# The two ends of a long VectorE-bound kernel: last blocks on four row groups, outputs with tokens on partitions, and another order of casts and transposes at the start

## The chip, the cores and the metric

One core of one Trainium2 chip (trn2). The metric is the device time of one execution in microseconds, the lower the better. Executions of one kernel mostly differ by one to three microseconds here (three of the kernel before took 723.6 to 725.4 us), so every comparison below is between executions taken in turn on the same chip. The "span" is the time from the first to the last instruction of a profiled execution. The device time is about 2 us longer.

"E" is the end of the 132 full multiplies of the last batch. It splits the run into a start (to the first multiply), a middle (first multiply to E) and an end (E to the end of the span).

## The reference

Four batches of 12,416 tokens with 128 channels. In each batch 32 inducing vectors attend to the tokens, which gives h. The tokens then attend to h, and the result goes through a gated feed-forward layer with 1,536 hidden units.

```python
def mab(q, kv):
    s = scale * (q @ kv.transpose(0, 2, 1))
    s = s - s.max(-1, keepdims=True)
    a = np.exp(s)
    a /= a.sum(-1, keepdims=True) + 1e-09
    return a @ kv
h = mab(I, x)            # 32 x 128 for each batch
y = mab(x, h)            # 12416 x 128 for each batch

gate = np.maximum(y @ w_gate, 0.0)
val = y @ w_val
out = gate * val @ w_out
```

## The kernel before

The tokens' attention has only 32 columns, so the kernel never forms y. It multiplies h with the two weights once for each batch (`hgv`, 32 rows of gate and 32 of value, each held twice on the partitions). Then it forms gate and value for 512 tokens (a "block") and 128 hidden units with matmuls of only 32 rows (K=32). The exponentials `p2` are the moving operand. They are left unnormalised: gate and value each carry the factor of the softmax's sum, so the output is scaled by 1/sum twice.

A "pair" is two blocks, and a "slot" is one 128-unit tile of one pair. In a slot TensorE makes two gate and two value tiles, ScalarE takes the ReLU of the gates, VectorE multiplies gate by value out of PSUM (one 128x1024 multiply), and TensorE does the output matmuls of an earlier block. A batch has 12 pairs of 12 slots, and one tile of 128 tokens is left over (the remainder: three half-size multiplies). In the last batch the remainder stands ahead of the last pair.

The exponentials of four blocks come from one "quad": a PSUM bank whose four row groups hold one block each, one exponential, and four small transfers that spread the result:

```python
    def s2_quad_exp(ps):
        p2q = st([P, BLK], FP16, "p2q", 2)
        nc.scalar.activation(out=p2q, in_=ps, func=AF.Exp, scale=sm_scale)
        return p2q

    def p2_copies(p2q):

        p2 = [st([P, BLK], FP16, "p2", 4) for _ in range(2)]
        for j in range(2):
            for d in range(2):
                nc.sync.dma_start(
                    out=p2[j][64 * d : 64 * d + 64, :], in_=p2q[64 * j : 64 * j + 64, :]
                )
        return p2
```

In the last pair of the whole run both blocks' values sit in the same row groups, and the output is formed with channels on partitions, copied, transposed by TensorE and scaled:

```python
for u in range(NFF):
    k = u // 6
    yield dict(
        mm=[
            [
                (...,                       # (cut)
                    p2[r : r + 32, :],
                    hgv[r : r + 32, :],
                )
                for d in range(2)           # both matmuls on the row group r
            ]
            for r in (32 * k, 64 + 32 * k)  # gates, values
        ],
        ...
    )

def step(i):                                # last_block: 12 matmuls of 512 columns
    if i == 0:
        c["ps"] = bank(tag, "o_ps")
    nc.tensor.matmul(c["ps"], wo[:, i, :], gv(i), start=(i == 0), stop=(i == NFF - 1))

def evac(at):
    ...                                     # (cut) copy to fp16 in two halves
    extra[at + 1].append(lambda: finish(zz, oT, osb))

def finish(zz, oT, osb):
    for a in (0, h):
        ps = bank("g", "oo_ps", [P, h, P], FP16)
        for t in range(h):
            nc.tensor.transpose(ps[:, t, :], oT[:, (a + t) * P : (a + t + 1) * P], eye16)
        ...                                 # (cut) scale each tile, store the half
```

At the start, the first batch's x comes in 14 parts. Each is cast to fp16 half by GpSimd and half by ScalarE (the one-tile part by VectorE), transposed by TensorE, and used for the scores and for h. The weights' transfers stand behind x in the same queue, and GpSimd casts them.

The softmax here doesn't subtract the row's maximum and nothing guards it: scores larger than these inputs give would overflow.

Of the kernel before, what the change touches and what calls it, by code (L numbers as in the profile page):

```python
# [18 lines left out]
def kernel(  # L19
# [20 lines left out]
    P = 128  # L40
# [131 lines left out]
    def s2_pair_pe(hT, xT, pr):  # L172
        ps = bank("g", "s2_ps")
        for r in range(4):
            nc.tensor.matmul(
                ps[32 * r : 32 * r + 32, :],
                hT[:, 0:M],
                xTs(xT, (2 * pr + r % 2) * TPB, TPB),
                start=True,
                stop=True,  # L180
            )
        return ps

    def s2_pair_exp(ps):
        p2 = st([P, BLK], FP16, "p2", 4)
        nc.scalar.activation(out=p2, in_=ps, func=AF.Exp, scale=sm_scale)
        return p2

    def s2_quad_pe(hT, xT, qd):

        ps = bank("g", "s2_ps")
        for r in range(4):
            nc.tensor.matmul(  # L193
                ps[32 * r : 32 * r + 32, :],
                hT[:, 0:M],
                xTs(xT, (4 * qd + r) * TPB, TPB),
                start=True,
                stop=True,
            )
        return ps  # L200
# [6 lines left out]
    def p2_copies(p2q):  # L207

        p2 = [st([P, BLK], FP16, "p2", 4) for _ in range(2)]
        for j in range(2):  # L210
            for d in range(2):
                nc.sync.dma_start(
                    out=p2[j][64 * d : 64 * d + 64, :], in_=p2q[64 * j : 64 * j + 64, :]
                )
        return p2
# [57 lines left out]

    for j in range(n_parts + 3):
        if j < n_parts:
# [3 lines left out]
            if t1 == NT:  # L279
                nc.vector.tensor_copy(out=dst, in_=x32)  # L280
            else:
                h = (t1 - t0) // 2
                nc.gpsimd.tensor_copy(out=dst[:, 0:h, :], in_=x32[:, 0:h, :])  # L283
                nc.scalar.copy(out=dst[:, h:, :], in_=x32[:, h:, :])  # L284
        if 1 < j < n_parts + 2:
# [28 lines left out]
        if j < n_parts:  # L314
            t0, t1 = parts[j]
            ps = bank("g", "xT_ps", [P, 8, P], FP16)
            for t in range(t0, t1):
                nc.tensor.transpose(ps[:, t - t0, :], x16[:, t, :], eye16)  # L318
            nc.vector.tensor_copy(out=xTs(xT, t0, t1 - t0), in_=ps[:, 0 : t1 - t0, :])  # L319
# [11 lines left out]
    s2 = s2_pair_pe(hT, xT, 0)  # L331
    p2 = s2_pair_exp(s2)
# [40 lines left out]
    def ev_s2_pair(b, pr, first, last):  # L373
        def pe(at):
            ps = s2_pair_pe(state[b]["hT"], state[b]["xT"], pr)

            def act():
                p2s[(b, pr)] = s2_pair_exp(ps)

            post[at + 1].append(act)  # L380
            ev_z2(lambda: p2s[(b, pr)], [(b, pr, k) for k in range(2)], TPB, at + 2)
# [3 lines left out]
    def ev_s2_quad(b, qd, first, last):  # L385
        def pe(at):
            ps = s2_quad_pe(state[b]["hT"], state[b]["xT"], qd)
# [71 lines left out]
    for b in range(B):  # L459
        for qd in range(NPAIR // 2):  # L460
            base = slot(b, 2 * qd, 0)
            if base:

                a = base - 2 * NFF if qd else slot(b - 1, NPAIR, 0) - 14
                ev_s2_quad(b, qd, a + 4, a + 8)
            else:
                ev_s2_pair(b, 1, 5, 8)
# [165 lines left out]
    def chain(w, gv, key, k, t0, first):  # L633
# [43 lines left out]
        if w == BLK:  # L677
            steps = [(first if i == 0 else 0, lambda i=i: step(i)) for i in range(NFF)]
            fast = key[0] == B - 1 and key[1] > NPAIR - 5
            counts = (5, 5) if fast else (6, 5)  # L680
# [6 lines left out]
    extra = defaultdict(list)  # L687

    def last_block(gv, key, k, t0, tag, on_act):
        c = {}  # L690
        h = TPB // 2

        def step(i):
            if i == 0:
                c["ps"] = bank(tag, "o_ps")
            nc.tensor.matmul(c["ps"], wo[:, i, :], gv(i), start=(i == 0), stop=(i == NFF - 1))  # L696

        def evac(at):
            z = z2is[key + (k,)][:, :, 0]
            zz = st([P, TPB], FP32, "zz", 2)  # L700
            nc.vector.tensor_tensor(out=zz, in0=z, in1=z, op=ALU.mult)
            oT = st([P, BLK], FP16, "oT", 4)
            osb = st([P, TPB, P], FP32, "osb", 4)
            for a in (0, h):
                nc.scalar.copy(out=oT[:, a * P : (a + h) * P], in_=c["ps"][:, a * P : (a + h) * P])
            extra[at + 1].append(lambda: finish(zz, oT, osb))

        def finish(zz, oT, osb):
            for a in (0, h):
                ps = bank("g", "oo_ps", [P, h, P], FP16)  # L710
                for t in range(h):
                    nc.tensor.transpose(ps[:, t, :], oT[:, (a + t) * P : (a + t + 1) * P], eye16)
                for t in range(h):
                    sc = zz[:, a + t : a + t + 1]
                    if on_act:
                        nc.scalar.activation(
                            out=osb[:, a + t, :], in_=ps[:, t, :], func=AF.Copy, scale=sc
                        )
                    else:
                        nc.vector.tensor_scalar(  # L720
                            out=osb[:, a + t, :],
                            in0=ps[:, t, :],
                            scalar1=sc,
                            scalar2=None,
                            op0=ALU.mult,
                        )
                nc.sync.dma_start(
                    out=ov[key[0]][:, t0 + a : t0 + a + h, :], in_=osb[:, a : a + h, :]
                )

        return step, evac
# [3 lines left out]
    def units():  # L735
        for b in range(B):
            for pr in order(b):
                base = slot(b, pr, 0)
                p2, hgv = p2s[(b, pr)], state[b]["hgv"]
                if (b, pr) == (B - 1, NPAIR - 1):  # L740
                    gvs = [st([P, 6, 2, BLK], FP16, "gv", 4) for _ in range(2)]
                    for k in range(2):
                        step, evac = last_block(
# [4 lines left out]
                            "og"[k],  # L748
                            k == 0,
                        )  # L750
                        if k == 0:
                            steps = [(base + 8, lambda i=i, f=step: f(i)) for i in range(NFF)]
                            job(steps, evac, ([3, 3, 3, 3],) * 2)
                        else:
                            for i in range(NFF):
                                a = base + 12 + (i + 2) // 4
                                extra[a].append(lambda i=i, f=step: f(i))
                            extra[base + 15].append(lambda f=evac: f(base + 16))
                    for u in range(NFF):
                        k = u // 6  # L760
                        yield dict(
# [8 lines left out]
                                    for d in range(2)  # L770
                                ]
                                for r in (32 * k, 64 + 32 * k)
                            ],
                            dst=gvs[k][:, u % 6, :, :].rearrange("p k c -> p (k c)"),
                        )
                elif pr < NPAIR:
# [14 lines left out]
                    for s in range(NFF):  # L791
                        if s % 6 == 0:
# [14 lines left out]
                            dst=gvs[-1][:, s % 6, :, :].rearrange("p k c -> p (k c)"),  # L807
                        )
# [49 lines left out]
    while True:  # L858
# [4 lines left out]
        if not (unit or any(window) or ready or fills or post or jobs or extra):  # L863
# [7 lines left out]
        if ready and at >= 10:  # L871
# [5 lines left out]
        if ready and at < 10:  # L877
# [46 lines left out]
        for f in extra.pop(at, []):  # L924
            f()
# [5 lines left out]
        if ready:  # L931
            n = ready["dst"].shape[-1]
            nc.vector.tensor_tensor(  # L933
                out=ready["dst"], in0=ready["g16"][:, 0:n], in1=ready["v"][:, 0:n], op=ALU.mult
            )
# [31 lines left out]
```

## Time and profile before

| | before |
|---|---|
| device time, median of 3 runs | 719.7 us (718.93 to 719.73) |
| span of the profiled execution | 716.4 us |
| first multiply starts | 28.67 us |
| 132 full multiplies of the last batch | 149.48 us, 1.132 us each |
| E to the last multiply's end | 18.26 us |
| E to the end of the span | 24.15 us |

The profile's page gives busy time by engine and then groups of equal instructions. The timeline gives runs of equal instructions of one engine in order: start, length, engine, source line, operation, tiles, count, and in brackets the idle time before and what ended it. It draws equal instructions into one line over waits shorter than 0.15 us, so a line without a bracket can still hold short waits. The last table row is what the change aims at: 24.15 us in which VectorE is not at its own pace or is done. The first multiply's start is its other aim. The lines themselves are in the prediction.

### The profile page before, as it was taken

How to read it: one execution, taken by the hardware profiler on the slowest of the kernel's cores; microseconds unless marked ns; L12 is line 12 of the kernel's file. 1: busy time of each engine (PE TensorE's matmuls, PEld its weight loads, DVE VectorE, ACT ScalarE, POOL GpSimd, SP SyncE). 2: the span in 40 equal slices, each digit the busy share in tenths (PEclk: the TensorE clock that was granted, in tenths of full speed). 3: DMA queues.
4: the chain of work that ended last, by engine and by line, in shares of the span. 5: the costliest groups of instructions: out<-in, count | busy, mean ns of one | idle time of the engine just before them, and what ended most of it. 6: DMA issues, size and time to landing. Idle time of an engine off the chain costs nothing.

```text
span 716.4 us, 13907 instructions
## 1 busy us (share of the span) xinstructions
PE 639.5 (89%) x4554; PEld 191.1 (27%) x4554; DVE 684.5 (96%) x630; ACT 679.6 (95%) x1378; POOL 343.3 (48%) x621
## 2 busy tenths in 40 slices
PE   5999999998988999998898999999888898898997
PEld 5422222222222222222222222222222222222222
DVE  4699999999999999999999999999999999999996
ACT  5799999999999999999999999999999999999985
POOL 3574536561365546626163662754325451551531
PEclk9999999999999999999999999999999999999999
DMA  9656677531346978522147766762122133232222
GB/s 344 219 125 177 150 181 163 103 89 45 91 126 166 195 164 223 126 67 76 46 107 206 170 155 170 170 118 75 59 68 83 56 90 67 67 88 67 67 68 72
DMA packets 142489, 87.76 MB, mean 122 GB/s; under 512 B 116913, under 2 KB 125905, under 8 KB 140113
## 3 DMA queue, kind: packets, MB, share of 16 engines
q1 hardware_dynamic: 142416, 86.88, 46.8%
q8 instruction: 35, 0.57, 0.3%
q14 instruction: 38, 0.30, 0.1%
HBM read 27.80 MB, written 25.43 MB: 74 GB/s over the span
## 4 chain that ended last, share of the span: by engine, by line
PE 44%; ACT 23%; issue 15%; DVE 15%; DMA 3%; SPq 0%; POOL 0%; DVEq 0%; ACTq 0%
PE o_ps L640 19%; ACT g L930 16%; DVE gv L933 14%; PE v_ps L830 14%; PE g_ps L830 7%; ACT oT L646 6%; DMA gv<-in_x_dram 2%; PE s_ps L193 1%; PE o_ps L696 1%; PE s1T_ps L511 1%; ACT p1T L521 0%; PE idle_ps L272 0%; DMA p1g<-p1T 0%; ACT hgv L166 0%; PE xT_ps L318 0%
## 5 line engine op out<-in xcount | busy, mean ns | idle before, releaser
L933 DVE TENSOR_TENSOR gv<-g,v_ps 128x1024 f16<-128x1024 f16 x576 | 660.8, 1213 | 10.7 <-PE g_ps L830 6.8
L930 ACT ACTIVATE g<-g_ps 128x512 f16<-128x512 f32 x1164 | 613.3, 620 | 16.6 <-PE g_ps L830 8.6
L640 PE MATMUL o_ps<-gv,wo 128*128 128x512 f16 x1128 | 339.8, 383 | 36.8 <-ACT oT L646 36.6
L657 POOL TENSOR_SCALAR osb<-o,z2i 128x128 f32<-128x128 f16 x380 | 164.6, 447 | 275.0 <-DMA o<-oT 251.3
L830 PE MATMUL g_ps<-p,hgv 32*128 32x512 f16 x1152 | 284.8, 380 | 5.3 <-ACT g L930 1.7
L830 PE MATMUL v_ps<-p,hgv 32*128 32x512 f16 x1152 | 226.2, 383 | 11.5 <-DVE gv L933 9.7
L830 PEld LDWEIGHTS <-hgv 32*128 32x128 f16 x2400 | 73.6, 91 | 271.5 <-issue 267.3
L640 PEld LDWEIGHTS <-wo 128*128 128x128 f16 x1176 | 79.2, 97 | 192.0 <-issue 169.1
L436 POOL TENSOR_TENSOR z2i<-zt,minus 128x16 f32<-128x16 f32 (+2 forms) x29 | 72.5, 2501 | 1.5
L646 ACT CAST oT<-o_ps 128x512 f16<-128x512 f32 (+1 forms) x98 | 57.1, 583 | 0.4 <-PE o_ps L640 0.4
L490 POOL CAST x<-x 128x2048 f16<-128x2048 f32 x18 | 34.0, 1890 | 19.4 <-DMA x<-in_x_dram 15.0
L429 POOL TENSOR_TENSOR zt<-zt 128x128 f32<-128x128 f32 (+5 forms) x116 | 33.4, 288 | 9.1
L595 POOL TENSOR_TENSOR hp<-hp,hq 128x129 f32<-128x129 f32 (+1 forms) x18 | 8.2, 457 | 32.5 <-ACT hq L594 27.9
L429 POOL TENSOR_TENSOR zt<-p2T 128x256 f32<-128x256 f16 (+2 forms) x29 | 17.0, 586 | 9.3 <-DMA p2T<-p2q 7.0
L319 DVE COPY xT<-xT_ps 128x1024 f16<-128x1024 f16 (+1 forms) x13 | 8.5, 650 | 7.2 <-PE xT_ps L318 6.4
L204 ACT ACTIVATE p2q<-s_ps 128x512 f16<-128x512 f32 x23 | 15.1, 656 | 0.0
L283 POOL CAST x<-gv 128x512 f16<-128x512 f32 (+1 forms) x13 | 7.5, 580 | 12.3 <-DMA gv<-in_x_dram 12.2
L284 ACT CAST x<-gv 128x512 f16<-128x512 f32 (+1 forms) x13 | 7.5, 580 | 6.1 <-DMA gv<-in_x_dram 6.1
L521 ACT ACTIVATE p1T<-s1T_ps 128x512 f16<-128x512 f32 x18 | 12.2, 677 | 0.0
L318 PE MATMUL xT_ps<-eye,x 128*128 128x128 f16 x97 | 9.6, 256 | 2.1 <-POOL x L283 1.5
L193 PE MATMUL s_ps<-xT,hT 128*32 128x512 f16 x92 | 9.2, 387 | 1.9
L291 ACT ACTIVATE p<-s_ps 128x256 f16<-128x256 f32 (+2 forms) x14 | 5.0, 354 | 4.9 <-PE s_ps L289 4.8
(90 smaller groups left out, 162.1 us busy)
## 6 DMA issues: line engine op xcount, KB each, us to landing
out_dram<-osb SPq DMA_DIRECT2D x94, 256.0 KB, 2.2
x<-in_x_dram SPq DMA_DIRECT2D x18, 1024.0 KB, 5.8
p<-p2q SPq DMA_DIRECT2D x92, 64.0 KB, 2.0
gv<-in_x_dram SPq DMA_DIRECT2D x11, 512.0 KB, 7.5
o<-oT SPq DMA_TRANSPOSE x98, 2.3
x<-in_moe_w_out_dram SPq DMA_DIRECT2D x1, 768.0 KB, 9.1
gv<-in_x_dram SPq DMA_DIRECT2D x2, 256.0 KB, 10.7
x<-in_moe_w_gate_dram SPq DMA_DIRECT2D x1, 512.0 KB, 9.2
```

Of the source, the lines that this page charges most:

```text
L193: nc.tensor.matmul(ps[32 * r : 32 * r + 32, :], hT[:, 0:M], xTs(xT, (4 * qd + r) * TPB, TPB), start=True, stop=True,)
L204: nc.scalar.activation(out=p2q, in_=ps, func=AF.Exp, scale=sm_scale)
L429: nc.gpsimd.tensor_tensor(out=dst, in0=v[:, :, :, 0:m], in1=v[:, :, :, m : 2 * m], op=ALU.add)
L436: nc.gpsimd.tensor_tensor(out=z2i, in0=v[:, :, :, 0], in1=minus1[:, 0 : n * g].rearrange("p (n g) -> p n g", n=n), op=ALU.pow,)
L490: nc.gpsimd.tensor_copy(out=s["x16"][:, t0:t1, :], in_=s["x32", q])
L521: nc.scalar.activation(out=p1T, in_=ps, func=AF.Exp, scale=sm_scale)
L640: nc.tensor.matmul(c["ps"][:, 0:w], wo[:, i, :], gv(i), start=(i == 0), stop=(i == NFF - 1))
L646: nc.scalar.copy(out=oT[:, 0:w], in_=c["ps"][:, 0:w])
L657: nc.gpsimd.tensor_scalar(out=osb[:, t, :], in0=o16[:, t, :], scalar1=zz, scalar2=zz, op0=ALU.mult, op1=ALU.mult,)
L830: nc.tensor.matmul(ps[:, cols], hgv[:, s * P : (s + 1) * P], p2, start=True, stop=True)
L930: nc.scalar.activation(out=g16[:, k * BLK : (k + 1) * BLK], in_=ps, func=AF.Relu)
L933: nc.vector.tensor_tensor(out=ready["dst"], in0=ready["g16"][:, 0:n], in1=ready["v"][:, 0:n], op=ALU.mult)
```

## The change

Its intent:

1. **Four row groups in the last pair.** Each of the last two blocks is laid out on all four row groups, so the two gates and two values of a slot can run at once. To get that layout without transfers, the last quad becomes three banks with three exponentials.
2. **Tokens on partitions.** The last two blocks' outputs take gv as the stationary operand (four matmuls of 128 columns in place of one of 512). The result needs no transposition, only scaling: GpSimd scales the first block, VectorE the second with two multiplies.
3. **The start.** The last part of x is cast by GpSimd alone and transposed earlier. A filler matmul follows each of the first twelve parts, to keep TensorE's clock up. The first multiply is split in two, and its value matmuls are issued ahead.
4. **"Even last chains".** The output matmuls of the blocks before the last ones are spread over 6 slots rather than 5, except those of the very last such block, which are done in 4.

```diff
@@ the last quad of p
-                ev_s2_quad(b, qd, a + 4, a + 8)
+                if b == B - 1 and qd == NPAIR // 2 - 1:
+                    bl = 2 * NPAIR - 4
+                    ev_s2(b, (b, 2 * qd), (bl, bl + 1, bl, bl + 1), a + 4, a + 8)
+                    for k in range(2):
+                        ev_s2(b, (b, 2 * qd + 1, k), (bl + 2 + k,) * 4, a + 16 + 6 * k, a + 20 + 6 * k)
+                else:
+                    ev_s2_quad(b, qd, a + 4, a + 8)
@@ the last pair's matmuls
-                                    for d in range(2)
+                                    for d, r in ((0, 64 * j), (1, 64 * j + 32))
                                 ]
-                                for r in (32 * k, 64 + 32 * k)
+                                for j in range(2)
                             ],
@@ the last two blocks' outputs
-            nc.tensor.matmul(c["ps"], wo[:, i, :], gv(i), start=(i == 0), stop=(i == NFF - 1))
+            for t in range(TPB):
+                nc.tensor.matmul(
+                    c["ps"][:, t, :],
+                    gv(i)[:, t * P : (t + 1) * P],
+                    wo[:, i, :],
+                    start=False,
+                    stop=(i == NFF - 1 and t == TPB - 1),
+                )
... (cut: copies, scaling and stores of the two blocks)
@@ the start
+            if j == n_parts - 2:
+                t0, t1 = parts[j + 1]
+                nc.gpsimd.tensor_copy(out=x16[:, t0:t1, :], in_=x32s[j + 1])
...
+        if j < n_parts - 1:
+            turn(j)
+        if j == n_parts - 2:
+            turn(j + 1)
+        elif j < n_parts - 2:
+            idle(z1_ps[:, BLK : 2 * BLK], 1, xTs(xT, parts[0][0], 4).rearrange("p t c -> p (t c)"))
@@ the multiply
+            w = n // ready.get("parts", 1)
+            for a in range(0, n, w):
+                nc.vector.tensor_tensor(...)      # parts=2 in slot 0 and in the very last slot
@@ chains
-            fast = key[0] == B - 1 and key[1] > NPAIR - 5
-            counts = (5, 5) if fast else (6, 5)
+            counts = (6, 5)
+            if key[0] == B - 1 and key[1] == NPAIR - 2:
+                counts = (6, 5) if k == 0 else (4, 4)
```

## The prediction

> **What bounds the kernel now.** I read the page's busy times first, then the groups, then VectorE in order of time, and last the two ends of the run.
>
> ```profile
> PE 639.5 (89%) x4554; PEld 191.1 (27%) x4554; DVE 684.5 (96%) x630; ACT 679.6 (95%) x1378; POOL 343.3 (48%) x621
> L933 DVE TENSOR_TENSOR gv<-g,v_ps 128x1024 f16<-128x1024 f16 x576 | 660.8, 1213 | 10.7 <-PE g_ps L830 6.8
> L930 ACT ACTIVATE g<-g_ps 128x512 f16<-128x512 f32 x1164 | 613.3, 620 | 16.6 <-PE g_ps L830 8.6
> ```
>
> VectorE does one multiply per slot, 576 in all, and waits 10.7 us before them in the whole run. ScalarE's 95% is less tight than it looks: ten ReLUs in a row took 5.00 us at the start (timeline from 27.42 us), so (5.00 - 0.60) / 9 = 0.49 us each, 0.98 us a slot. VectorE in order of time settles it:
>
> ```profile
> 542.76 149.48 DVE L933 TENSOR_TENSOR gv<-g,v_ps 128x1024 f16<-128x1024 f16 x132 [0.58 <-PE g_ps L830]
> 692.16 0.68 DVE L933 TENSOR_TENSOR gvr<-g,v_ps 128x512 f16<-128x512 f16 x1
> 693.10 1.28 DVE L933 TENSOR_TENSOR gvr<-g,v_ps 128x512 f16<-128x512 f16 x2 [0.26 <-PE g_ps L830]
> 695.16 8.75 DVE L933 TENSOR_TENSOR gv<-g,v_ps 128x1024 f16<-128x1024 f16 x7 [0.78 <-ACT g L930]
> 704.27 3.81 DVE L933 TENSOR_TENSOR gv<-g,v_ps 128x1024 f16<-128x1024 f16 x3 [0.36 <-PE g_ps L830]
> 708.15 2.35 DVE L933 TENSOR_TENSOR gv<-g,v_ps 128x1024 f16<-128x1024 f16 x2
> ```
>
> The last batch's 132 multiplies run without a gap: (149.48 - 1.21) / 131 = 1.132 us a slot, VectorE's own pace. Nothing in the change makes that multiply cheaper, and it is over 90% of the span. Only the two ends can give: before the first multiply (28.67 us), and from 692.25 us (end of the 132), when the one-tile remainder and the last pair of blocks run. There the slot is longer: 12 multiplies from 695.16 to 710.50 us are 15.34 us, 1.28 us each.
>
> The reason for 1.28 is on TensorE, and after the last multiply a chain follows:
>
> ```profile
> 695.66 0.38 PE L830 MATMUL v_ps<-p,hgv 32*128 32x512 f16 x1
> 695.89 0.37 PE L830 MATMUL v_ps<-p,hgv 32*128 32x512 f16 x1
> 696.20 0.82 PE L640 MATMUL o_ps<-gv,wo 128*128 128x512 f16 x3
> 710.14 1.46 PE L696 MATMUL o_ps<-gv,wo 128*128 128x512 f16 x6
> 711.63 0.65 ACT L705 CAST oT<-o_ps 128x256 f16<-128x256 f32 x2 [0.22 <-PE o_ps L696]
> 712.44 1.13 DVE L720 TENSOR_SCALAR osb<-oo_ps,zz 128x128 f32<-128x128 f16 x4 [1.87 <-PE oo_ps L712]
> 713.08 0.85 SPq L727 DMA_DIRECT2D out_dram<-osb  x2
> ```
>
> The two value matmuls share a row group and start 0.23 us apart, as the gates do. So the four take 0.54 us (695.66 to 696.20), the three output matmuls 0.75, a slot 1.29. In a slot of the pair before, all four started at 684.64 and the outputs at 684.97: 0.33 us, slot 1.08. The last matmuls end at 711.60, 1.10 us after the last multiply; copy, transposes, scaling and store then take 4.8 us to 716.4.
>
> **What the Trainium skill says.** (1) "TensorE: Matmul & The Clock Gate", Part 3 (packing small matmuls): K=32 matmuls in different row groups run concurrently, in one row group they don't; the trace agrees, 0.33 against 0.54 us. (2) Same page, "Back-to-back issue gap": 56 ns for an isolated 128-column matmul, about 81 in a sustained stream with weight loads. The change swaps 12 512-column matmuls for 48 128-column ones, so this decides. Here the remainder's output matmuls took 0.38 us for 4 and 0.62 for 8: 60 ns each with its weight load. I use 56 to 60. (3) "VectorE: DVE Perf Modes", the perf-mode tier table: a tensor_tensor with a PSUM operand gets the 1x mode, so 1,024 elements at that page's 0.96 GHz are 1.07 us; the trace's 1.13 agrees. (4) The first page again, Part 1: TensorE falls to half clock after an idle window of about 3.4 us. The trace grants 0.50 over 21 to 23 us, after 1.28 us of idle that ended at 18.78.
>
> **The change part by part.**
>
> *Start.* The last quarter-megabyte of x is cast wholly by GpSimd (0.61 instead of 0.40 us in parallel), ScalarE loses a 0.40 us cast, and the part's transposes move ahead of the scores of the part before. Filler matmuls (0.22 us each) after each part may keep TensorE at full clock. hT_ps now ends at 25.0. Following the order, the reshuffle alone brings that to about 24.4, with the full clock about 23.8. But what follows needs w_val's second cast:
>
> ```profile
> 25.12 1.04 POOL L327 CAST wv<-x 128x1024 f16<-128x1024 f32 x1 [0.64 <-DMA x<-in_moe_w_val_dram]
> 26.29 0.38 PE L156 MATMUL hgv_ps<-wv,hT 128*32 128x512 f16 x2
> 27.19 1.28 DVE L340 CAST hgv<-hgv_ps 128x512 f16<-128x512 f32 x2
> ```
>
> It waits for a transfer and ends at 26.16; the matmuls that read it start at 26.29 now, so they can move by under 0.1 us. The gain left lies behind them: VectorE's first copies (0.75 us) can now be done before 26.3, so the second copies start at about 26.7 to 26.9 instead of 27.19. The first multiply, split in two and with its values issued earlier, need not sit out the 0.21 us for ScalarE. Two halves cost about 0.07 more than one (two 128x512 multiplies took 1.28, one whole 1.21). Net: 0.30 to 0.50 + 0.2 - 0.07, I take **0.45 us**. The rest of the 0.6 to 1.2 us becomes idle time before the weights.
>
> *Middle.* The last quad of p becomes three exps in place of one: two more on ScalarE, about 0.55 us each, while their DMA copies go. ScalarE's spare time is 1.13 - 0.98 = 0.15 us a slot, less one 0.5 us copy every six slots: 0.07 net, near 5 us over the last 70 slots. Spreading chains over 6 slots instead of 5 changes nothing where VectorE has no gap. Cost 0 to 0.3 us, I take **0.1 lost**.
>
> *Remainder and last pair.* Let E be the end of the last full multiply, 692.25 now. The first of the last pair starts at E + 2.91. In the new order each remainder slot has 2 output matmuls instead of 3, then 3, and the chain's next matmul waits for ScalarE's copy of the single output bank, which stands behind two ReLUs. Laying the slots out I get E + 2.8, so 0.1 saved. With four row groups a slot on TensorE is 0.33 + 0.75 = 1.08, or 0.33 + 12 x 0.056 + 0.1 = 1.10, just under VectorE's 1.132. Early on there are two slots of four output matmuls (1.30) and two more bank waits; I charge 0.8 us. So 11 x 1.132 + 1.28 (last one halved) + 0.8 = 14.5: the last multiply ends at E + 17.3, against E + 18.25 (710.50). **0.95 saved.**
>
> *After the last multiply.* The second block's chain can't start until the first block's sum has left the one output bank and the last value matmuls are issued, about 2.1 us before the last multiply ends. It needs 0.22 + 48 x 0.056 + 0.2 = 3.1 us: it ends 1.0 to 1.1 us after the last multiply. That equals the 1.10 of before. With tokens on partitions, two VectorE multiplies remain: 128x256 from PSUM, an estimate of 0.43 + 0.33 from hT's 0.23 us for 64 columns and the 1x pace. The first store is issued at +0.5, the second at +0.95 (0.43 each). Now the second store is issued near 713.5 and the span ends 2.9 us later; same size, same 2.9. So 0.95 + 2.9 = 3.85 instead of 4.8: **0.95 saved.** GpSimd's four scalings for the first block (0.60 each from fp32, as its one such instruction took) end about 0.5 us before they could block the last store.
>
> Sum: 0.45 - 0.1 + 0.95 + 0.95 = 2.25; the run-to-run spread of 0.8 us covers the rounding. **719.7 - 2.25 = 717.4 us**; I say 717.2, as the start is taken carefully.
>
> **Rivals.** *The start pays in full:* if the weights' transfers land earlier, since the last cast is moved, 0.6 to 1.2 us come through and the time is near 716. Against it: they wait in the same queue, and w_val's cast waits 0.64 us on it. *The last pair becomes perfectly VectorE-bound:* no bank waits, 0.8 us more, 716.3. For it: single waits under 0.6 us vanish in buffers in the steady part; against it: the chain of the second block has one bank. *TensorE becomes the bound:* at 81 ns a 12-matmul slot is 1.40 us, costing 0.27 x 4, and the final 48 cost 1.2 more: the tail gains nothing, 719.3. Against it are the 60 ns above. *GpSimd and the queue hold the last store:* the first block's store stands ahead of it in SyncE's queue, with 0.5 us of slack; if GpSimd is 1 us late, 718.
>
> **Range and chances.** Start 0 to 1.2, slots of the last pair 0 to 1.8, tail 0.3 to 1.5 saved; they are independent, so 715.4 to 718.8 should hold it 8 times in 10. Two per cent would be 14.4 us, which neither end contains: faster 0.01, within 0.98, slower 0.01.
>
> **What would show it.** First multiply near 28.2 instead of 28.67, with TensorE idle before the w_val matmuls. A gapless run of about 130 multiplies at 1.132 in the last batch. Last pair's multiplies at 1.13 to 1.2 instead of 1.28, no two matmuls of one slot 0.22 apart. 48 output matmuls in about 2.7 us; under 4 us from their end to the span's. I am wrong if the output matmuls take 80 ns, if gaps appear around the extra exps, or if the start moves by 1 us.

## The result, and the profile after

| | before | changed |
|---|---|---|
| device time, median of 4 runs each | 719.72 us (718.93 to 720.44) | 717.87 us (717.31 to 718.57) |
| span of the profiled execution | 716.4 us | 716.4 us |
| first multiply starts | 28.67 us | 28.67 us |
| first multiply to E | 663.57 us | 665.49 us |
| E to the last multiply's end | 18.26 us | 17.58 us |
| E to the end of the span | 24.15 us | 22.24 us |

The ratio is 0.9975, with a 95% interval of 0.9958 to 0.9992. Ratios are worked out from runs of the same rounds, so a ratio is not quite the ratio of the medians quoted beside it. The change gained 1.85 us by the medians. That is under 2% and so counts as "same", and it lies inside the predicted range.

The two profiled spans are equal by chance. The profiled execution of before took 718.67 us, less than any of the four timed ones. So I compare stages, not spans.

The page of the changed kernel, busy time by engine and the two costliest groups (the multiply is now L953, the ReLU L948):

```profile
PE 639.7 (89%) x4640; PEld 194.7 (27%) x4640; DVE 683.8 (95%) x628; ACT 678.0 (95%) x1372; POOL 350.0 (49%) x639
L953 DVE TENSOR_TENSOR gv<-g,v_ps 128x1024 f16<-128x1024 f16 (+1 forms) x578 | 660.8, 1210 | 11.6 <-PE g_ps L849 8.1
L948 ACT ACTIVATE g<-g_ps 128x512 f16<-128x512 f32 x1164 | 613.1, 619 | 17.3 <-PE g_ps L849 9.4
```

VectorE's multiply takes the same 660.8 us. The page can't show what the change did: idle time before the multiply went from 10.7 to 11.6 us, which alone would read as a loss. VectorE's timeline shows it better:

```profile
28.67 5.81 DVE L953 TENSOR_TENSOR gv<-g,v_ps 128x512 f16<-128x512 f16 x6
...
544.16 150.00 DVE L953 TENSOR_TENSOR gv<-g,v_ps 128x1024 f16<-128x1024 f16 x132 [0.58 <-PE g_ps L849]
...
697.07 8.61 DVE L953 TENSOR_TENSOR gv<-g,v_ps 128x1024 f16<-128x1024 f16 x7 [0.58 <-PE g_ps L849]
705.93 5.81 DVE L953 TENSOR_TENSOR gv<-g,v_ps 128x1024 f16<-128x1024 f16 x6 [0.25 <-issue]
712.73 0.76 DVE L723 TENSOR_TENSOR osb<-o_ps,zz 128x256 f32<-128x256 f32 x2 [1.00 <-issue]
```

Three things are to be seen. The first multiply starts when it did before. The 132 multiplies take 150.00 us, not 149.48. The last pair (now 13 multiplies, as the very last is halved) starts 2.91 us after E and ends 17.58 us after it, with a gap of 0.25 us inside whose releaser is "issue", which means that no wait is seen. The end, TensorE's and SyncE's timeline:

```profile
705.08 0.39 PE L849 MATMUL v_ps<-p,hgv 32*128 32x512 f16 x2
705.40 0.84 PE L709 MATMUL o_ps<-wo,gv 128*128 128x128 f16 x12
706.18 0.39 PE L849 MATMUL v_ps<-p,hgv 32*128 32x512 f16 x2
...
709.79 2.85 PE L709 MATMUL o_ps<-wo,gv 128*128 128x128 f16 x48
...
713.18 0.81 SPq L729 DMA_DIRECT2D out_dram<-osb  x2
```

The values of a slot now start together (0.39 us for two, no second group 0.23 us behind). Twelve output matmuls take 0.84 us, and the slot comes round after 706.18 - 705.08 = 1.10 us, just under VectorE's 1.132. The 48 output matmuls of the last block end at 712.64, 0.90 us after the last multiply (697.07 + 14.67 = 711.74). Two scalings and the two stores follow, and nothing else.

At the start, VectorE and TensorE of the changed kernel:

```profile
17.43 0.61 PE L265 MATMUL xT_ps<-eye,x 128*128 128x128 f16 x8
17.87 0.38 PE L259 MATMUL z_ps<-xT,eye 128*128 128x512 f16 x1
...
18.60 0.61 PE L265 MATMUL xT_ps<-eye,x 128*128 128x128 f16 x8
...
24.24 1.04 POOL L324 CAST wv<-x 128x1024 f16<-128x1024 f32 x1 [0.29 <-DMA x<-in_moe_w_val_dram]
...
25.33 0.36 DVE L142 RECIPROCAL rz<-z_ps 128x32 f32<-128x32 f32 x1 [1.05 <-PE hT_ps L310]
...
26.52 0.38 PE L156 MATMUL hgv_ps<-wv,hT 128*32 128x512 f16 x2
```

One part takes TensorE 18.60 - 17.43 = 1.17 us, of which the filler (L259, 0.22 us from issue to issue) is a fifth. The reciprocal that follows h's last matmul starts at 25.33 us. In before it started at 25.10:

```profile
25.10 0.36 DVE L142 RECIPROCAL rz<-z_ps 128x32 f32<-128x32 f32 x1 [1.05 <-PE hT_ps L313]
```

So h is not earlier but 0.23 us later (and that with the last part of x 0.49 us sooner: its cast starts at 20.29 us, in before at 20.78), although the windows show the full clock that the fillers were meant for. The columns are the window, its length, then busy time and count of PE, PEld, DVE, ACT and POOL, the granted TensorE clock, the DMA share and GB/s. First before, then changed:

```profile
20.00:22.00 2.00, 1.91 (x30) 1.85 (x31) 0.82 (x2) 1.15 (x5) 1.37 (x4) 0.53 1.02 404
22.00:24.00 2.00, 1.99 (x40) 1.74 (x39) 1.13 (x3) 0.78 (x3) 1.25 (x3) 0.62 1.11 329
```

```profile
20.00:22.00 2.00, 2.00 (x47) 1.74 (x45) 1.10 (x2) 1.28 (x4) 1.61 (x4) 1.00 1.02 401
```

Before ran at 0.53 and 0.62 of the clock just where it matters and was still done sooner.

**Half-clock stretches blur everything.** Such a stretch lasts 3.41 us in each trace that has one. It also comes in the middle of a run, at places that differ between traces. In the changed kernel's trace it stands at 253.8 us. Laid slot by slot over a trace without one, it costs 1.27 us (1.25 to 1.29 in six traces). Take it off, and "first multiply to E" is 665.49 - 1.27 = 664.22 us: 0.65 us longer than before, not 1.92.

### The profile page after: what moved, and what is told of

Same layout as the page of the kernel before. It is cut to its first block, busy times and chain, and to the rows that moved or that the text cites. A ratio compares the mean times of both kernels' runs of the same rounds, so it can differ in the third digit from the quotient of the medians.

```text
span 716.4 us, 14081 instructions
## 1 busy us (share of the span) xinstructions
PE 639.7 (89%) x4640; PEld 194.7 (27%) x4640; DVE 683.8 (95%) x628; ACT 678.0 (95%) x1372; POOL 350.0 (49%) x639
## 5 line engine op out<-in xcount | busy, mean ns | idle before, releaser
L953 DVE TENSOR_TENSOR gv<-g,v_ps 128x1024 f16<-128x1024 f16 (+1 forms) x578 | 660.8, 1210 | 11.6 <-PE g_ps L849 8.1
L948 ACT ACTIVATE g<-g_ps 128x512 f16<-128x512 f32 x1164 | 613.1, 619 | 17.3 <-PE g_ps L849 9.4
L436 POOL TENSOR_TENSOR z2i<-zt,minus 128x16 f32<-128x16 f32 (+3 forms) x31 | 73.4, 2367 | 1.6
L429 POOL TENSOR_TENSOR zt<-zt 128x32 f32<-128x32 f32 (+5 forms) x124 | 35.1, 283 | 9.7
L429 POOL TENSOR_TENSOR zt<-p2T 128x256 f32<-128x256 f16 (+3 forms) x31 | 17.5, 564 | 16.3 <-DMA p2T<-p2q 7.7
L175 PE MATMUL s_ps<-xT,hT 128*32 128x512 f16 x108 | 10.8, 387 | 2.4
L953 DVE TENSOR_TENSOR gvr<-g,v_ps 128x512 f16<-128x512 f16 x12 | 8.0, 684 | 1.7 <-PE g_ps L849 1.7
```

The source lines that it names most:

```text
L175: nc.tensor.matmul(ps[32 * r : 32 * r + 32, :], hT[:, 0:M], xTs(xT, blocks[r] * TPB, TPB), start=True, stop=True,)
L429: nc.gpsimd.tensor_tensor(out=dst, in0=v[:, :, :, 0:m], in1=v[:, :, :, m : 2 * m], op=ALU.add)
L436: nc.gpsimd.tensor_tensor(out=z2i, in0=v[:, :, :, 0], in1=minus1[:, 0 : n * g].rearrange("p (n g) -> p n g", n=n), op=ALU.pow,)
L948: nc.scalar.activation(out=g16[:, k * BLK : (k + 1) * BLK], in_=ps, func=AF.Relu)
L953: nc.vector.tensor_tensor(out=ready["dst"][:, a : a + w], in0=ready["g16"][:, a : a + w], in1=ready["v"][:, a : a + w], op=ALU.mult,)
```

## The experiments

Three batches of four kernels, five rounds each. "Clear runs" are executions with a mean granted clock of at least 0.999. This is a cut of mine, and few runs fall in it. Of before, 5 of 33 were clear, with a mean of 718.22 us; the other 28 had 720.19. Of the changed kernel, 5 of 10 were clear (717.56), and the other 5 had 718.33.

| run | median (lowest to highest), us | ratio to before, 95% | clear runs: number, mean us | E to end, us |
|---|---|---|---|---|
| e0_changed_again | 717.94 (717.54 to 718.46) | 0.9963, 0.9934 to 0.9993 | see above | 22.22 |
| e1_start_only | 720.54 (719.04 to 721.80) | 1.0004, 0.9971 to 1.0036 | none | 24.17 |
| e2_end_only | 717.56 (717.36 to 718.23) | 0.9958, 0.9929 to 0.9988 | none | 22.09 |
| e3_no_filler | 717.93 (715.97 to 719.19) | 0.9960, 0.9929 to 0.9991 | 2, 716.57 | 22.24 |
| e4_old_outputs | 718.40 (717.82 to 719.62) | 0.9980, 0.9961 to 0.9999 | 4, 718.33 | 22.73 |
| e5_old_groups | 719.18 (718.16 to 720.38) | 0.9989, 0.9970 to 1.0008 | 2, 718.40 | 23.72 |
| e7_early_exps | 718.08 (717.62 to 718.61) | 0.9973, 0.9953 to 0.9993 | 3, 717.79 | 22.20 |
| e8_no_split | 717.84 (717.17 to 718.39) | 0.9970, 0.9952 to 0.9988 | 3, 717.37 | 22.14 |
| f1_late_filler | 717.45 (715.97 to 718.13) | 0.9975, 0.9962 to 0.9988 | 2, 716.24 | 22.15 |
| f2_copied_blocks | 716.93 (715.75 to 717.31) | 0.9967, 0.9955 to 0.9980 | 1, 715.75 | 22.13 |
| f3_copied_old_start | 716.00 (715.34 to 716.99) | 0.9958, 0.9945 to 0.9971 | 4, 715.83 | 22.12 |
| f4_one_more | 717.77 (717.25 to 718.59) | 0.9985, 0.9972 to 0.9999 | 3, 717.51 | 22.26 |

Before's median in the same rounds was 719.89 us for e0 to e3, 719.86 for e4 to e8 and 718.93 for f1 to f4 (11 runs each). It moved by nearly 1 us between batches, so medians of different batches are not compared. "E to end" is E, taken from VectorE's timeline, subtracted from the end of the profiled span. The page prints the span to 0.1 us, so this column is good to 0.05 us.

### The changed kernel once more

No edit.

> The changed kernel, unaltered, on the same chip and in the same rounds as the others, for a second trace. It should be 1.85 us below the kernel before, as the first comparison gave, give or take 0.6. If the long slots of batches 1 to 3 in its first trace (0.74 us at 255 us, 0.57 at 189, 0.56 at 412) belong to the change, they stand again at the same multiplies (numbers 194, 137, 328); if they are chance, they don't.

717.94 us, again 1.95 us below before. The stages repeat: 132 multiplies in 150.01 us and the last multiply 17.58 us after E. Of the three long slots, those of 0.57 and 0.56 us stand again at the same multiplies, so they belong to the change. The one of 0.74 us does not: it was the half-clock stretch, which is there again, but now at 425 us.

### The start alone

```diff
+ before.py, with the new order of casts and transposes, the fillers,
+ the early values and the split first multiply; the end as before
```

> The kernel before with the start of the change alone. My prediction's step: 0.45 us saved, first multiply near 28.2 us, bounded by the cast of w_val. Rival, from the changed kernel's trace: the filler matmuls make TensorE the bound of the start (1.17 us a part), which takes the saving back: 0.0 us, give or take 0.3, first multiply near 28.7.

The ratio is 1.0004, but its interval is some 2 us wide to each side, too wide to tell 0.45 us from nothing. The trace decides for the rival: the first multiply starts at 28.75 us (28.67 in before) and the reciprocal at 25.41 us (25.33 in the changed kernel, 25.10 in before).

### The end alone

```diff
  the changed kernel, with
- the new order at the start, the fillers, the early values, the split
+ the start of before
```

> The changed kernel with the start of the kernel before. If the start gives nothing, this saves all of the 1.85 us (1.4 to 1.9, with the two exps' 0.5 us in it). If my prediction's 0.45 us for the start holds, it is that much slower than the whole change. In its trace the end of the last multiply should be 17.6 us after the end of the 132 full ones, and the span's end 4.7 us later.

717.56 us, the lowest median of its batch: the times show no part of the gain in the start. By luck its profiled execution kept the full clock at the start, and VectorE's timeline shows the start of before as I had expected it of the change, and the last pair without a wait of 0.15 us or more:

```profile
28.18 8.15 DVE L941 TENSOR_TENSOR gv<-g,v_ps 128x1024 f16<-128x1024 f16 x7 [0.28 <-ACT g L936]
...
696.42 14.33 DVE L941 TENSOR_TENSOR gv<-g,v_ps 128x1024 f16<-128x1024 f16 x13 [0.58 <-PE g_ps L838]
```

The first multiply is at 28.18 us with none of the change's start in it. Its reciprocal came at 24.22 us, and VectorE then waited 0.21 us for the matmuls on w_val's second half. So at full clock w_val's cast does set the first multiply, as predicted, once h is early enough. The changed start, with 28.67 and 28.62 us in its two traces, is a loss of 0.5 us against this.

### No fillers

```diff
-        elif j < n_parts - 2:
-            idle(z1_ps[:, BLK : 2 * BLK], 1, xTs(xT, parts[0][0], 4)...)
```

> The changed kernel without the 12 filler matmuls of the start; all else as in the change. If the fillers bound the start, parts go at the pace of the transfers and the first multiply comes 0.3 to 0.7 us earlier than with them (near 28.1). If they pay because they hold the full clock, TensorE is granted 0.5 from about 20 to 23.5 us again and the start is no earlier or up to 0.5 us later.

The median equals the changed kernel's (717.93 against 717.94), but the spread is wide: 715.97 to 719.19. The two clear runs have 716.57 us, 1.0 less than the changed kernel's clear runs. The profiled one has half the clock from 20.0 to 23.4 us, as before has it, and a reciprocal at 26.18. Its last part of x also came later than in the changed kernel (the cast starts at 21.75 us, not 20.29), so only the time from there can be compared: 4.43 us to the reciprocal here and 4.32 in before, both with the half clock; 4.05 to 5.32 in the eight traces with all fillers, which have none. In two of these, e0 and e4, GpSimd waited for a part of x about as long as in before (1.99 and 1.90 us against 2.01), and the full clock held. So the fillers do prevent the half-clock stretch, and cost about as much as it does.

### Four row groups, outputs as before

```diff
  the changed kernel, with
- last_block: gv stationary, tokens on partitions
+ last_block of before: 512-column matmuls, copy, transposes, scaling
```

> The changed kernel with the last pair on four row groups but its outputs made as before (twelve 512-column matmuls, copy, transposes, scaling). My prediction gives the row groups 0.95 us and the new output path 0.95 us of their own. So: the last pair's multiplies go at 1.13 to 1.2 us a slot, the last one ends 17.2 to 17.6 us after the end of the 132 full ones, but the span ends 5.9 us after that (23.3 after the 132; 22.2 in the change, 24.15 before): about 0.95 us slower than the change. Rival, that the two are worth nothing apart because the output copies hold ScalarE and the banks: 24 us after the 132, 1.8 slower.

E to the end takes 22.73 us, against 24.15 before: the row groups, with the halved last multiply, bring 1.42 us. The last multiply ends 17.47 us after E, as expected; the rest takes 5.26 us and not the expected 5.9.

### New outputs, row groups as before

```diff
  the changed kernel, with
- three banks and exponentials for the last four blocks, r = 64 * j, 64 * j + 32
+ ev_s2_quad and its transfers, both matmuls of a tile on the row group r
```

> The changed kernel with the last pair's p in the old layout (both gates in one row group, both values in another) and the new outputs with tokens on partitions. By my prediction the slot stays at 0.54 + 0.75 us = 1.28 to 1.3, the last multiply ends 18.3 us after the 132, and the span 4.7 us later: 23.0, about 0.8 us slower than the change. The 132 run without the 0.5 us of long slots, if the two extra exps cause these, so the time comes out only 0.3 us above the change.

E to the end takes 23.72 us, where 23.0 was expected: the outputs, again with the halved last multiply, bring 0.43. The two parts together bring 1.91, and 1.42 + 0.43 = 1.85. That looks as if they simply added, but the halved multiply is in both sums, and no run takes it out. The last multiply is *later* than before here, 18.63 us after E against 18.26 (18.3 expected). TensorE's and VectorE's timelines of this run's last pair show why the outputs alone don't pay there:

```profile
704.42 0.38 PE L841 MATMUL v_ps<-p,hgv 32*128 32x512 f16 x1
...
705.73 0.39 PE L841 MATMUL v_ps<-p,hgv 32*128 32x512 f16 x1
...
705.49 5.81 DVE L945 TENSOR_TENSOR gv<-g,v_ps 128x1024 f16<-128x1024 f16 x6 [0.48 <-PE g_ps L841]
```

A slot on TensorE takes 705.73 - 704.42 = 1.31 us, still longer than VectorE's multiply, and VectorE waits 0.48 us on gates. The middle tells something else: with the quad's one exponential back and the new counts kept, the 132 multiplies take 149.54 us. So the half microsecond comes with the three banks, and not with the chains spread over six slots. Each of the two extra banks brings an exponential and four more score matmuls on TensorE; no run takes these apart.

### The two extra exponentials earlier

```diff
-                        ev_s2(b, (b, 2 * qd + 1, k), (bl + 2 + k,) * 4, a + 16 + 6 * k, a + 20 + 6 * k)
+                        ev_s2(b, (b, 2 * qd + 1, k), (bl + 2 + k,) * 4, a + 10 + 6 * k, a + 14 + 6 * k)
```

> The changed kernel with the two last blocks' scores and exps six slots earlier. If the extra exps, standing close to the remainder's exp and the output copies, make the long slots of the last batch (150.0 us for the 132 multiplies instead of 149.5), the 132 come back to 149.5 to 149.7 and the time falls by 0.3 to 0.5 us. If their number counts and not their place, 150.0 stays. If the chains of 4 output matmuls cause it, the long slots stay near the start of the last full pair.

The 132 multiplies take 150.00 us in both places. By the rule set beforehand their number would count and not their place, but the traces say more. Laid multiply by multiply over a trace with one exponential (the copied blocks, below), each trace shows where it falls behind. ScalarE's timeline of the changed kernel, then of this run:

```profile
670.42 0.67 ACT L186 ACTIVATE p<-s_ps 128x512 f16<-128x512 f32 x1
677.49 0.67 ACT L186 ACTIVATE p<-s_ps 128x512 f16<-128x512 f32 x1
```

```profile
664.14 0.67 ACT L186 ACTIVATE p<-s_ps 128x512 f16<-128x512 f32 x1
671.21 0.67 ACT L186 ACTIVATE p<-s_ps 128x512 f16<-128x512 f32 x1
```

In the changed kernel the first of the two, twelve slots after the exponential before it, delays nothing. The multiplies come late from the 119th to the 130th: behind the second, six slots after the first, and behind the remainder's short one, six slots after that (0.46 us in all). In this run both stand six slots after another, and the late ones are the 107th to the 118th. The remainder's, now twelve slots behind, delays nothing. So what costs in these traces is an exponential six slots after another, and not their number. No run sets them all twelve apart.

### The first multiply whole

```diff
-                            parts=2 if base + s == 0 else 1,
```

> The changed kernel with its very first multiply whole again; the filler matmuls stay. Two multiplies (numbers 138 and 329) started 0.36 us late in all four traces with the changed start and in neither without; they lie 384 VectorE instructions apart, and the split is one instruction more. If that shift of one exposes a pause in the supply of instructions, both late starts vanish: 0.7 us faster, less the split's own worth (0.0 to 0.2). If the fillers or the early turn cause them, they stay and the time is unchanged.

The profiled execution has no half-clock stretch, and the last pair takes one unbroken run:

```profile
190.15 8.20 DVE L952 TENSOR_TENSOR gv<-g,v_ps 128x1024 f16<-128x1024 f16 x7 [0.21 <-PE g_ps L848]
...
696.58 14.33 DVE L952 TENSOR_TENSOR gv<-g,v_ps 128x1024 f16<-128x1024 f16 x13 [0.58 <-PE g_ps L848]
```

The last multiply ends 17.24 us after E instead of 17.58. At 190 us, the multiply that waits 0.57 us in the changed kernel waits 0.21 here; before has 0.21 too. The times do not show it (in the profiled execution GpSimd waited 3.00 us for an early part of x, and the first multiply came only at 29.63 us): 717.84 us against 718.08 of the run with early exponentials and 717.94 of the changed kernel, and 717.37 against 717.56 in the clear runs.

### One more instruction, nothing split

The split can matter in two ways: as two halves, or as one more VectorE instruction ahead of all others. This tells them apart.

```diff
-                            parts=2 if base + s == 0 else 1,
+    spare = constp.tile([P, 1], FP16, name="spare")
+    nc.vector.memset(spare, 1.0)          # among the constants
```

> The changed kernel without the split of the first multiply (whose run had no late multiplies), plus one tiny VectorE instruction (a memset of one column) among the constants at the very start. Theory: the split hurts only because it is one more VectorE instruction, which shifts all later ones, so that a pause of 0.36 us that recurs every 384 VectorE instructions falls in front of a multiply's start instead of behind a running one. Then multiplies 138 and 329 are 0.36 us late again and the last pair takes 17.58 us from E instead of 17.24, though nothing is split; time about 1 us more than without the split on a quiet chip, within the spread 717.8 to 718.6. Rival: it is the split itself, the two halves and their order; then no late multiplies and 17.24 us.

The timeline of VectorE:

```profile
189.81 8.01 DVE L954 TENSOR_TENSOR gv<-g,v_ps 128x1024 f16<-128x1024 f16 x7 [0.57 <-ACT p2q L193]
...
705.02 5.81 DVE L954 TENSOR_TENSOR gv<-g,v_ps 128x1024 f16<-128x1024 f16 x6 [0.25 <-issue]
```

The late multiplies are back, 0.36 us each, and the last multiply ends 17.58 us after E, with nothing split. So the count does it, not the halves. Multiplies 138 and 329 are VectorE's records 320 and 704 in the trace, 384 apart. Laid slot by slot over the run without the split, this kernel falls behind from its twentieth multiply on in six steps, at records 320, 448, 704, 832, 1088 and 1216, which are 128 or 256 apart.

The size that I had expected in the time, about 1 us, was too large. The first of the pauses leaves 0.17 us, the second is made good within ten multiplies, about 0.06 comes at multiply 520, and only the last one stays whole, 0.34. As this kernel is 0.18 us quicker over its first twenty multiplies, it is 0.45 us behind at the last one.

### Fillers only from the eighth part on

```diff
-        elif j < n_parts - 2:
+        elif 6 < j < n_parts - 2:
             idle(...)
-                            parts=2 if base + s == 0 else 1,
```

> The changed kernel without the split of the first multiply, and with filler matmuls only from the eighth part of x on (five fillers instead of twelve). Theory: the early fillers run at the cold clock, put TensorE behind the transfers, and from then on it never catches up (1.17 us a part against 0.96 without); the late ones alone hold the full clock at no cost, as a part then takes 1.18 us against the 1.28 us in which its transfer comes. Then rz starts before 25.0 us, the second cast of w_val becomes the bound, and the first multiply starts 2.9 us after that cast's end (28.2 us if the transfers come as in the changed kernel), with no half clock between 16 and 28 us. Without the split no multiply starts 0.36 us late at numbers 138 and 329, and the last pair takes 17.24 us from E. Time 716.7 to 717.5 us. Rival: the fillers have nothing to do with it and rz stays at 25.3; then 717.8, as without the split alone.

The reciprocal and the first multiply come 1.12 and 0.80 us earlier than in the changed kernel, at full clock from 16 to 28 us:

```profile
24.21 0.36 DVE L142 RECIPROCAL rz<-z_ps 128x32 f32<-128x32 f32 x1 [1.05 <-PE hT_ps L310]
...
27.87 18.65 DVE L952 TENSOR_TENSOR gv<-g,v_ps 128x1024 f16<-128x1024 f16 x16 [0.20 <-ACT g L947]
```

The rival, that fillers have nothing to do with it, falls. Nor was it the transfers: from the start of the last cast of x to the reciprocal it is 3.71 us here, and 4.05 to 5.32 in the eight traces with all fillers. The old order without fillers, where the full clock held, takes 3.50 us (the end alone), so the early casts and transposes of the change gain nothing either. The first multiply starts 2.19 us after the end of w_val's cast (25.68), where I had expected 2.9, which was too much. 717.45 us is inside the expected 716.7 to 717.5. The two clear runs have 716.24, against 717.37 without the split alone.

### One exponential and ten transfers for the last four blocks

```diff
+                for key, src in (
+                    ((b, 2 * qd), (0, 64, 64)),
+                    ((b, 2 * qd + 1, 0), (64, 96, 32)),
+                    ((b, 2 * qd + 1, 1), (96, 128, 32)),
+                ):
+                    lo, hi, n = src
+                    p2s[key] = st([P, BLK], FP16, "p2", 5)
+                    for d in range(P // n):
+                        nc.sync.dma_start(out=p2s[key][n * d : n * d + n, :], in_=q[lo:hi, :])
```

on top of the late fillers and the whole first multiply.

> As the run with late fillers, but the last four blocks get one exponential again, and ten small transfers lay it out on the row groups (four before). Theory: the two extra exponentials on ScalarE are what lengthened the 132 full multiplies of the last batch from 149.5 to 150.0 us; then the 132 take 149.5 again, and the time is 0.4 us below the run with late fillers. Rival: the six extra transfers make some multiply wait, or the half microsecond comes from somewhere else; then the 132 stay at 149.9 to 150.0.

```profile
542.20 149.47 DVE L957 TENSOR_TENSOR gv<-g,v_ps 128x1024 f16<-128x1024 f16 x132 [0.58 <-PE g_ps L853]
```

149.47 us, as before the change, and no wait from the extra transfers. 716.93 us is 0.52 below the run with late fillers, where 0.4 was expected (six and five runs, with overlapping spreads).

### The same with the start of before

> The end of the change with the start of before (no split, no fillers), and the last four blocks laid out by ten transfers from one exponential. If the start is worth nothing in the sum and the exponentials are worth 0.45 us: 132 multiplies in 149.5 us, last pair 17.24 us from E, time about 717.1 us, 0.45 below the run that had the end of the change alone (717.56). If it is no better than 717.6, the half microsecond does not reach the time.

716.00 us is lower than I expected (717.1); most of that surprise is that the whole batch was quicker, before by 0.95 us. Its 132 multiplies take 149.48 us and the last one ends 17.26 us after E. It is the best kernel. Against before its ratio is 0.9958, with an interval that lies below that of the run with one more instruction, which behaves like the changed kernel and was timed in the same rounds (0.9972 to 0.9999). Four of its five executions were clear. The new start with late fillers (716.93) is not better than this. The intervals of the two overlap, so I don't say that it is worse.

## Why the prediction was right or wrong

**Right, as a class and as a range.** 717.87 us measured, 717.2 predicted, 715.4 to 718.8 the range. Three of its errors (start, exponentials, split) point the same way, against the change, and the range covers them. That the sum came out so near is partly luck: 0.45 us of the gain lies outside the span, in no term of the prediction, and stands in for the start that failed. The steps in turn:

**The start: wrong.** "They can move by under 0.1 us ... Net ... I take **0.45 us**" became 0. I had looked for the bound behind h, in w_val's cast, and took from the order that h itself would be at 23.8 to 24.4 us. The cast was indeed earlier, it ended at 25.28, and did not bind. h was late, because I booked the fillers as free ("may keep TensorE at full clock"). They are not. Here TensorE goes from one part to the next without a gap, and each part costs it 1.17 us, 0.22 of that for the filler. The early ones take even longer (0.59 to 0.63 us at 8.5 to 10 us in the trace, 0.38 later); TensorE falls behind the transfers and doesn't catch up. That the fillers did it is shown by the run with late ones only: the reciprocal moves from 25.33 to 24.21 us at the same clock, and w_val's cast then binds as predicted. The earlier h that I had booked for the reshuffle itself (24.4 us) is in no trace: at full clock the old order has it at 24.22, the new one with late fillers at 24.21. The clock that the fillers were to hold, they did hold.

**The middle: wrong in size.** "Cost 0 to 0.3 us, I take **0.1 lost**" became 0.52, of which 0.05 is the shift by one below and 0.47 comes with the exponentials. The mechanism was named (three exponentials for one on an engine with little to spare), and taking the extra two out brings it back: 149.47 us in the copied blocks against 149.95. What failed is how I counted ScalarE's spare time: 0.07 us a slot, summed over 70 slots. By the prediction's own 0.07 us a slot, six slots hold 0.42 us and twelve 0.84 (an estimate), and an exponential takes 0.67. That fits the traces, in which one six slots after another delays multiplies and one twelve slots after does not. It was not tested further, and the extra score matmuls are not told apart.

**The split: wrong, a part that was not in the sum.** I booked 0.07 us for the second half of the first multiply. In the traces it costs some 0.45 us (the times don't resolve it), by shifting all later instructions of VectorE by one, as the run with one more memset shows. The trace of before, without that instruction, does not show it.

**Remainder and last pair: right in kind, 0.27 too high.** "E + 17.3 ... **0.95 saved**": measured 17.58, 0.68 saved. Without the shift by one it is 17.24, 1.02 saved, so the slots were estimated right (1.10 us on TensorE, as predicted), and the missing 0.3 is the pause at 705 us. Of the 0.8 us charged for the early slots, 0.6 are there: 14.33 us for the pair, where VectorE's own pace would give 11 x 1.132 + 1.28 = 13.73. The one-tile remainder did not get quicker: 2.91 us instead of 2.92, predicted 2.8.

**After the last multiply: right, 0.28 too low.** 0.95 saved was predicted and 1.23 measured (5.89 to 4.66 us). The chain ended 0.90 us after the last multiply and not 1.0 to 1.1, the 48 matmuls took 2.85 us with their latency (predicted "about 2.7"), and the two scalings 0.76 (predicted 0.43 + 0.33). The run with the old outputs has 22.73 - 17.47 = 5.26 us there, so 0.63 of the 1.23 is there without the new outputs. In that run the last six output matmuls start 0.93 us before the last multiply ends (709.81 us against 710.74), in before 0.36 us. Which part of the change brings that forward, the row groups or the halved multiply, no run shows. GpSimd's four scalings took 1.75 us together, 0.44 each and not 0.60, and never stood in the way.

**The sum.** 0.45 - 0.1 + 0.95 + 0.95 = 2.25 was predicted. The traces give 0 - 0.65 (0.47 for the exponentials, the rest mostly the shift) + 1.91 = 1.26 in the span, half-clock stretches in the middle taken off. A further 0.45 us lies outside the span: device time less span is 2.24 us before and 1.78 changed, in clear runs and others alike. It was 2.23 in the run with the start only and 1.80 with the end only, so it belongs to the end (1.94 with the old outputs, 2.0 in the two kernels with ten transfers); what makes it is open. Together 1.7, beside 1.85 to 1.95 in the medians. The clear runs alone show less, 0.66 us (5 runs each, from different batches), and the others 1.86. So part of the gain of the medians comes with how many executions are hit by half-clock stretches: 28 of 33 before, 5 of 10 changed, by their mean clock. Whether the change causes that, or chance, these counts can't settle.

**The rivals.** "TensorE becomes the bound" at 81 ns a matmul is out: 12 in 0.84 us. "The start pays in full" is out. "The last pair becomes perfectly VectorE-bound" is out too: even without the shift the 13 multiplies take 14.33 us, 0.6 more than VectorE's pace. GpSimd did not hold the last store. (The 1.07 us of the prediction's point 3 on the skill is an estimate from the page's clock; the trace has 1.13.)

## What to carry to other kernels

Before you call a filler or an extra instruction free, look whether its engine has a gap at that place: a filler on an engine that runs part after part without one delays everything behind it. At a bound of one engine for over 90% of the time, lay two traces over each other instruction by instruction; sums by group and spans hid here that a gain of 1.9 us at the end was partly given back by two small losses in the middle. Count an engine's spare time between two pieces of extra work, not over the whole stretch: here twelve slots hid an exponential and six did not. And undo each part of a change on its own: the best kernel keeps its end, with one exponential for the last four blocks, and drops the rest.

## What the Trainium skill lacked or had wrong

- "TensorE: Matmul & The Clock Gate", "Back-to-back issue gap", gives about 81 ns for a sustained 128-column matmul with its weight load. Here 48 in a row took 2.85 us with the last one's latency, 59 ns each at most. The page's isolated figure (56 ns) was the better guide.
- The same page, Part 1, has the half clock come after an idle window of about 3.4 us, and further down tells of a kernel in which short idle times bring it, without saying how much idleness is needed. Here it came at the start of before behind a wait of 1.28 us, and six traces have it in mid-run with TensorE busy for 2.60 of the 3.41 us ahead of it. Busy time alone does not decide: in the changed kernel's trace the 3.41 us up to 253.82 us, with 2.60 busy, are followed by the half clock, and those up to 566.81 us, with 2.47 busy, are not. Each stretch cost 1.25 to 1.29 us in a run bound by VectorE; the page's figures are for kernels of another kind.
- "Runtime: NRT & Kernel Launch", "Instruction fetch mechanics", says that instructions are streamed in blocks and that crossing a boundary is mostly hidden. Pauses of up to 0.36 us on VectorE, 128 or 256 trace records apart, came and went with a single memset. That it is the instruction supply would fit; no run shows its source.
- No page that I read has a time for GpSimd's scaling by a per-partition scalar from fp32 in SBUF, 128x128: 1.75 us for four here, 0.44 us each, as quick as from fp16 (0.45 us in the mean of 380).
